# Attention and gated feed-forward on one core: x quarters on VectorE, sums tied to TensorE's order, and attention shifted between two phases

## The chip, the cores and the metric

The kernel runs on one core of one Trainium2 chip. The metric is device time in microseconds (us) of one execution. A core has TensorE (matrix products), VectorE, ScalarE and GpSimd, and SyncE, whose queue (SP) issues the transfers. Each engine executes its own instructions in the order in which they stand in the program; an instruction that has to wait holds back everything behind it on that engine. In the rows PE is TensorE, PEld its weight loads, DVE VectorE, ACT ScalarE, POOL GpSimd; SPq, PEq and so on are the queues that issue.

## The reference

```python
# attention over 8 batches, 8 heads, 576 positions of 64; keys and values averaged by 8 positions
k_p = k.reshape(B, H, Sp, 8, D).mean(axis=3)          # Sp = 72
v_p = v.reshape(B, H, Sp, 8, D).mean(axis=3)
scores = np.matmul(q, k_p.transpose(0, 1, 3, 2)) / np.sqrt(D)
scores = scores - np.max(scores, axis=-1, keepdims=True)
attn = np.exp(scores)
attn = attn / (np.sum(attn, axis=-1, keepdims=True) + 1e-09)
x = np.matmul(attn, v_p).transpose(0, 2, 1, 3).reshape(B * S, H * D)   # 4608 x 512
# feed-forward
h = x @ w_in                                          # 512 x 2048
g = h * np.clip(h + 3.0, 0.0, 6.0) / 6.0
out = g @ w_out                                       # 2048 x 512
```

## The kernel before

**Precision.** TensorE works in the float32r type. A number is split in a high part (a copy that rounds) and a low part (the number less the high part), and a product is made as high by high, high by low and low by high: three products for one. So each operand costs ScalarE a copy (`hi`) and VectorE a subtraction (`lo`).

**Blocks.** The 4608 tokens are worked off in blocks of 512, 256 and then 384 (`BLOCKS`). Blocks 0 to 3 are plain: for each of 16 chunks f of the hidden width, `Step.h` multiplies x by w_in (line 806, product `psh`), `relu` (814), `gate` (818), `hi` (822) and `lo` (826) make the gated value, and `Step.out` multiplies it by w_out (836, `pso`). `run` goes through these steps of a block with a lag of 2 between h and out; `hooks` adds work behind certain steps.

**Super blocks.** Blocks 4 to 11 go in pairs, as four super blocks. Their product by w_in uses a Strassen-like scheme of seven products instead of eight. It needs seven operands made of quarters of x, x1 to x7 (`x_ops`: `mix` adds or subtracts quarters of 128x768 elements, line 961, on GpSimd; `split` makes high and low parts, lines 952 and 953), and seven sums of quarters of w_in (`sums_of`, lines 902 to 910), which are made once, in blocks 2 and 3, and stored to DRAM. `plain_of` stores the other parts of the weights there. A super block then has two phases. In the *products phase* 56 products groups of six (line 1032, `psx`) run over the list N1; `keep` (1012) copies a result, `plus` (1007) adds one, and `gate` (1001, 1002) makes g. In the *out phase* g is split (`split_g`, lines 1018 and 1019) and multiplied by w_out (1077), 16 chunks f for six tiles t of 128 tokens; at the end each tile goes from PSUM into an `o` tile (1083) and to DRAM (1084). `next_w` loads weights of the products phase from DRAM, three chunks ahead in four buffers (932); `next_w2` those of the out phase, also in four buffers (938). In the last five chunks f of an out phase (`TAIL`) the x operands of the next super block are made.

**Attention.** While block j is multiplied, the attention of later blocks is computed in small steps, which `Paced` puts between the products, some per slot: `scores` (product 436, maximum 440, exponential 444, reciprocal 460 and 461, division on GpSimd 472 and 478), `transposes` (542 to 565; `ahi`, `alo`, `arem` are the split results), and the products with the values (`av`, 612), whose result a ScalarE copy (614) puts into x. Beside them stand the loads of queries (217), keys (224) and values (252, 257), and the sums over eight positions of keys (`prep_k`, 238) and values (`prep_v`, 356), on VectorE. A super block has `att_steps(j + 2)` in its products phase and `att_steps(j + 3)` in its out phase.

**What sets the order.** The program is written in one order and then placed engine by engine by a scheduler with a model of time of its own, which may move an instruction ahead of others that wait. Two things bind it: the table `ORDER` up to step 3 of block 1, and `behind`, which says that one instruction stands after another, without a wait at run time. Before, `behind` is used outside of the table in one place, the stores of plain weights: each stands behind the last TensorE instruction that had been written when it was written.

**Buffers.** Tiles of keys, values and queries, value sums and the output tiles `o` share one ring of four (`ring`). The tile `wq` of the weight sums exists once.

Of the kernel before, what the change touches and what calls it, by code (L numbers as in the profile page):

```python
# [89 lines left out]
def attention_moe_kernel(  # L90
# [72 lines left out]

    def put_in_order():

        a, b = window
        last = {}

        def on(i, engine):
            return i.engine == engine and (i.opcode == "DMACopy") == (engine == mybir.EngineType.SP)  # L170

        for name, text in ORDER.items():
            engine = getattr(mybir.EngineType, name)
            mine = [i for i in traced[a:b] if on(i, engine)]
            numbers = []
            for part in text.split():
                x, _, y = part.partition("-")
                numbers += range(int(x), int(y or x) + 1)
            assert sorted(numbers) == list(range(len(mine)))
            for x, y in zip(numbers, numbers[1:]):  # L180
                behind(mine[y], mine[x].name)
            last[engine] = mine[numbers[-1]].name
        for i in traced[b:]:
            if i.engine in last and on(i, i.engine):
                behind(i, last[i.engine])
# [42 lines left out]
    def prep_k(b, p):  # L228
# [11 lines left out]
        )  # L240
        if i == two:
# [104 lines left out]
    def prep_v(b, p):  # L346
# [11 lines left out]
        )  # L358
        if p == NPAIR - 1:
# [536 lines left out]
    def sums_of(i, h):  # L896
# [4 lines left out]
        for r, w in enumerate(pair_of(i)):  # L901
            nc.vector.tensor_tensor(  # L902
                out=q[:, 2 * r : 2 * r + 2], in0=w[:, 0, :, half], in1=w[:, 1, :, half], op=ALU.add
            )
        for to, a, b, how in ((0, 0, 2, ALU.subtract), (2, 2, 3, ALU.add), (3, 3, 0, ALU.subtract), (1, 1, 3, ALU.subtract)):
            nc.vector.tensor_tensor(out=q[:, to], in0=q[:, a], in1=q[:, b], op=how)  # L906
# [5 lines left out]
    def store(to, src):  # L912

        last = next(i for i in reversed(traced) if i.engine == mybir.EngineType.PE)
        nc.sync.dma_start(to, src)
        behind(traced[-1], last.name)
# [18 lines left out]
    def next_w2(n):  # L935
        while (m := len(loaded2)) <= n + 3 and m < len(supers) * NF:
            loaded2[m] = late[1].tile([P, 2, DM], F32R, name="ws2", bufs=4)
            nc.sync.dma_start(loaded2[m].bitcast(F32), w2_dram[m % NF])
        return loaded2[n]
# [3 lines left out]
    def x_ops(j):  # L943
# [15 lines left out]
        def mix(to, p, q, how):  # L959
            def make():  # L960
                nc.gpsimd.tensor_tensor(out=to(), in0=p(), in1=q(), op=how)
# [26 lines left out]
    def super_block(n, j, first_att, second_att):  # L988
# [9 lines left out]
        def gate(src, i, k):  # L998

            r = late[1].tile([P, HALF], F32, name="r", bufs=NREL)  # L1000
# [21 lines left out]
        for m, (i, o) in enumerate(N1):  # L1022
# [6 lines left out]
            paced.slot()  # L1029
            for c in range(2):  # L1030
# [28 lines left out]
        for f in range(NF):  # L1059
# [3 lines left out]
            for t in range(NT2):  # L1063
# [16 lines left out]
                o = ring("o")[:, :DM]  # L1080
# [220 lines left out]
    for n, step in enumerate(make):  # L1301
        j, u = (2, 3 + 2 * n) if n < 7 else (3, n - 7)
        hooks[j].setdefault(u, []).append(step)
# [16 lines left out]
    for n, j in enumerate(supers):  # L1320
        last = n == len(supers) - 1
        super_block(n, j, [] if last else att_steps(j + 2), [] if last else att_steps(j + 3))
# [46 lines left out]
```

## Time and profile before

| | |
|---|---|
| median of 3 runs | 928.28 us (927.34 to 930.86) |
| profiled execution | 928.58 us, of it 926.8 us span |
| TensorE busy | 893.1 us, 96% of the span |
| VectorE, ScalarE, GpSimd busy | 577.5, 512.2, 113.0 us |
| mean granted TensorE clock | 0.992 |
| moved by DMA | 172.63 MB, 186 GB/s in the mean |

The profiled execution took 928.58 us as a run; its span goes from the first instruction to the last. A busy TensorE isn't TensorE at its peak: products are pipelined, so the rows show a single product of 384 columns as 341 ns, while twelve in a row take little more than six times as long. Plain blocks end at about 362 us of the span, the four super blocks at about 507, 650, 795 and 927 us.

### The profile page before, as it was taken

The numbers are of one execution on the slowest core, as the hardware profiler recorded it, in microseconds if no ns is written. First come the engines' busy times: TensorE is split into PE (matmuls) and PEld (weight loads), VectorE is DVE, ScalarE is ACT, GpSimd is POOL, SyncE is SP. The second block draws the span as 40 slices with busy tenths as digits, with TensorE's granted clock in tenths as the row PEclk, the third lists the DMA queues.
The fourth block names the chain that finished last, engine by engine and source line by source line (L and its number), as shares of the span: only waits on it lengthen the run. The fifth ranks groups of instructions, "written<-read, shape, count | busy, mean of one in ns | idle before, by whom it ended". The sixth has DMA issues, their size and how long they took to land.

```text
span 926.8 us, 14062 instructions
## 1 busy us (share of the span) xinstructions
PE 893.1 (96%) x4760; PEld 801.4 (86%) x4760; DVE 577.5 (62%) x1167; ACT 512.2 (55%) x1473; POOL 113.0 (12%) x184
## 2 busy tenths in 40 slices
PE   7999999999999979899999999999999999999998
PEld 7788888899799878898888899888989888999786
DVE  6999846686867785867435886426676436454321
ACT  5998665665556465666323867423666534344221
POOL 4100002111101231001002201003110103000000
PEclk9999999999999999999999999999999999999999
DMA  9960205166549554976435976534966433775332
GB/s 302 392 249 0 92 12 178 46 192 202 169 129 343 181 159 165 337 242 216 160 114 172 335 260 227 165 114 135 325 210 214 161 116 114 257 232 192 114 119 108
DMA packets 93527, 172.63 MB, mean 186 GB/s; under 512 B 12048, under 2 KB 50704, under 8 KB 93456
## 3 DMA queue, kind: packets, MB, share of 16 engines
q1 hardware_dynamic: 93312, 171.74, 55.8%
q8 instruction: 38, 0.62, 0.3%
q14 instruction: 33, 0.27, 0.1%
q10 hardware_dynamic: 144, 0.00, 0.0%
HBM read 139.20 MB, written 32.51 MB: 185 GB/s over the span
## 4 chain that ended last, share of the span: by engine, by line
PE 67%; DVE 13%; DMA 11%; ACT 4%; SPq 3%; issue 2%; DVEq 0%; POOL 0%; ACTq 0%
PE psx L1077 28%; PE psx L1032 20%; PE psh L806 7%; PE pso L836 7%; DMA ws<-wd 3%; DMA wd<-wq 3%; PE psa L612 3%; PE psa L436 2%; DVE vsum L356 2%; ACT e L444 2%; SPq L910 2%; DVE wq L906 1%; DVE wq L902 1%; DMA kst<-k_l 1%; DMA raw<-w_in_l 1%
## 5 line engine op out<-in xcount | busy, mean ns | idle before, releaser
L1032 PE MATMUL psx<-x,ws 128*128 128x384 f32 x1344 | 255.9, 341 | 9.9 <-DMA ws<-wd 6.0
L1032 PEld LDWEIGHTS psx<-x,ws 128*128 128x128 f32 x1344 | 234.0, 190 | 16.0 <-DVE g L1007 4.2
L1077 PE MATMUL psx<-ws,ghi 128*128 128x512 f32 (+1 forms) x800 | 236.7, 384 | 1.6 <-DVE g L1002 1.6
L1077 PEld LDWEIGHTS psx<-ws,ghi 128*128 128x128 f32 x800 | 146.3, 188 | 28.7 <-DVE g L1002 2.1
L806 PE MATMUL psh<-xhi,w 128*128 128x384 f32 (+2 forms) x520 | 148.4, 343 | 5.0 <-DVE g L818 5.0
L1077 PE MATMUL psx<-ws,glo 128*128 128x512 f32 (+1 forms) x400 | 147.7, 382 | 0.0
L836 PE MATMUL pso<-w,ghi 128*128 128x512 f32 x384 | 121.6, 403 | 0.0
L1019 DVE TENSOR_TENSOR glo<-g,ghi 128x768 fp32r<-128x768 f32 x64 | 66.0, 1037 | 88.1 <-ACT ghi L1018 81.2
L806 PEld LDWEIGHTS psh<-xhi,w 128*128 128x128 f32 x520 | 94.4, 190 | 12.7 <-DVE g L818 5.9
L1018 ACT CAST ghi<-g 128x768 fp32r<-128x768 f32 x64 | 52.9, 835 | 82.4 <-PE psx L1077 80.4
L444 ACT ACTIVATE e<-psa,mx 128x72 f32<-128x72 f32 x256 | 78.8, 326 | 21.9 <-DVE mx L440 19.6
L806 PE MATMUL psh<-xlo,w 128*128 128x384 f32 (+2 forms) x260 | 88.1, 339 | 0.1
L1077 PEld LDWEIGHTS psx<-ws,glo 128*128 128x128 f32 x400 | 74.9, 188 | 14.2
L1001 ACT ACTIVATE r<-g,small 128x384 f32<-128x384 f32 x96 | 56.2, 614 | 43.7 <-DVE g L1007 42.9
L472 POOL TENSOR_TENSOR a<-e,sm 128x256 f32<-128x256 f32 x60 | 40.0, 669 | 327.3 <-DVE sm L461 237.4
L836 PEld LDWEIGHTS pso<-w,ghi 128*128 128x128 f32 x384 | 69.1, 190 | 10.4
L836 PE MATMUL pso<-w,glo 128*128 128x512 f32 x192 | 73.7, 398 | 0.0
L1007 DVE TENSOR_TENSOR g<-psx,c 128x384 f32<-128x384 f32 x96 | 53.0, 554 | 30.5 <-PE psx L1032 27.3
L1012 ACT COPY c<-psx 128x384 f32<-128x384 f32 x96 | 43.4, 486 | 23.3 <-PE psx L1032 22.7
L1002 DVE SCALAR_TENSOR_TENSOR g<-r,g 128x384 f32<-128x384 f32 x96 | 52.0, 570 | 4.7 <-ACT r L1001 4.6
L444 ACT ACTIVATION_READ_ACCUMULATOR e<-psa,mx 128x1 f32 x256 | 54.1, 211 | 0.0
L806 PEld LDWEIGHTS psh<-xlo,w 128*128 128x128 f32 x260 | 49.4, 190 | 4.4 <-DVE xlo L591 0.4
(120 smaller groups left out, 1194.0 us busy)
## 6 DMA issues: line engine op xcount, KB each, us to landing
ws<-wd SPq DMA_DIRECT2D x112, 512.0 KB, 4.3
ws<-w2d SPq DMA_DIRECT2D x64, 512.0 KB, 3.3
out<-o SPq DMA_DIRECT2D x35, 256.0 KB, 3.1
raw<-w_in_l SPq DMA_DIRECT2D x16, 512.0 KB, 8.5
raw<-w_out_l SPq DMA_DIRECT2D x16, 512.0 KB, 9.4
wd<-wq SPq DMA_DIRECT2D x64, 128.0 KB, 2.0
w2d<-w SPq DMA_DIRECT2D x16, 512.0 KB, 4.3
kst<-k_l SPq DMA_DIRECT2D x28, 288.0 KB, 4.9
```

The source lines that it names most:

```text
L444: nc.scalar.activation(self.e[:, h], self.ps[:, h], AF.Exp, bias=self.mx[:, h : h + 1], accum_out=self.sm[:, h : h + 1])
L472: engine.tensor_tensor(out=self.a[:, : 4 * D].rearrange("p (h s) -> p h s", h=4), in0=e[:, :, :D], in1=sm[:, :, None].broadcast_to([P, 4, D]),
L806: nc.tensor.matmul(self.ps, l[f][:, c, :], r[:, c, :], start=c == 0 and i == 0, stop=c == NCC - 1 and i == 2)
L836: nc.tensor.matmul(pos, l, r, start=f == 0 and i == 0, stop=f == NF - 1 and i == 2)
L1001: nc.scalar.activation(r, src, AF.Relu, bias=half_low, scale=GSCALE / (6.0 * WSCALE))
L1002: nc.vector.scalar_tensor_tensor(out=g_of[i][:, k], in0=r, scalar=GSCALE, in1=src, op0=ALU.min, op1=ALU.mult)
L1007: nc.vector.tensor_tensor(out=g_of[i][:, k], in0=ps, in1=kept, op=ALU.add)
L1012: nc.scalar.copy(c, ps)
L1018: nc.scalar.copy(hi, g)
L1019: nc.vector.tensor_tensor(out=lo, in0=g, in1=hi.bitcast(F32), op=ALU.subtract)
L1032: nc.tensor.matmul(ps, w[:, l, c * P : (c + 1) * P], t[:, r, c], start=o in (1, 2, 5) and c == 0 and k == 0, stop=c == 1 and k == 2, skip_ ...
L1077: nc.tensor.matmul(pos, l, w[:, r, cols], start=f == 0 and k == 0, stop=end and k == 2)
```

## The change

It has six parts.

1. `after_products` puts the instruction just written behind the last TensorE instruction written before it. It is called after each sum of keys (`prep_k`) and values (`prep_v`), after the first two adds of each sum of weights (`sums_of`), after the stores (as before) and after the loads of `next_w2`. It acts from step 3 of block 1 on.
2. The sums of weights are hooked to every second step of blocks 2 and 3, eight in each. Before, seven stood at steps 3, 5, ... 15 of block 2 and nine at steps 0 to 8 of block 3.
3. The quarters of x are mixed by VectorE instead of GpSimd.
4. The first loads of w_out for the first super block are written into its products phase, ahead of the first product of pair 6.
5. The outputs of a super block use buffers of `ghi2`, `glo2` and `r` (the last made wider for it), not the ring.
6. The attention steps of both blocks are joined, and the first 36% stand in the products phase, 64% in the out phase.

```diff
+    def after_products():
+        if len(window) == 2:
+            behind(traced[-1], next(i for i in reversed(traced) if i.engine == mybir.EngineType.PE).name)
...
@@ prep_k, prep_v: behind the tensor_reduce; sums_of: behind the tensor_tensor of line 902
+        after_products()
...
     def store(to, src):
-        last = next(i for i in reversed(traced) if i.engine == mybir.EngineType.PE)
         nc.sync.dma_start(to, src)
-        behind(traced[-1], last.name)
+        after_products()
...
             nc.sync.dma_start(loaded2[m].bitcast(F32), w2_dram[m % NF])
+            after_products()
...
-                nc.gpsimd.tensor_tensor(out=to(), in0=p(), in1=q(), op=how)
+                nc.vector.tensor_tensor(out=to(), in0=p(), in1=q(), op=how)
...
-            r = late[1].tile([P, HALF], F32, name="r", bufs=NREL)
+            r = late[1].tile([P, DM], F32, name="r", tag="ro", bufs=NREL)[:, :HALF]
...
             paced.slot()
+            if n == 0 and i == NPR - 2 and o == 1:
+                next_w2(0)
...
-                o = ring("o")[:, :DM]
+                tag, size = ("ro", DM) if t >= 4 else (("ghi2", "glo2")[t % 2], 2 * HALF)
+                o = late[1].tile([P, size], F32, name="o", tag=tag, bufs=3)[:, :DM]
...
-        j, u = (2, 3 + 2 * n) if n < 7 else (3, n - 7)
-        hooks[j].setdefault(u, []).append(step)
+        hooks[2 + n // NPR].setdefault(2 * (n % NPR), []).append(step)
...
-        super_block(n, j, [] if last else att_steps(j + 2), [] if last else att_steps(j + 3))
+        att = [] if last else att_steps(j + 2) + att_steps(j + 3)
+        cut = int(0.36 * len(att))
+        super_block(n, j, att[:cut], att[cut:])
```

What it does to the order shows at three places. The line numbers of the changed kernel are higher, by 7 to 10. VectorE at the change from block 1 to block 2, before: `vsum` are sums of values, `alo` low parts of transposed attention tiles.

```order
L826 TENSOR_TENSOR glo<-g,ghi 128x256
L356 TENSOR_REDUCE vsum<-vst 128x64 x3
L554 TENSOR_TENSOR alo<-psa,ahi 128x2x128
L818 SCALAR_TENSOR_TENSOR g<-g,psh 128x256
L554 TENSOR_TENSOR alo<-psa,ahi 128x2x128
L356 TENSOR_REDUCE vsum<-vst 128x64
```

The same place in the changed kernel (`mx` is the maximum of scores):

```order
L561 TENSOR_TENSOR alo<-psa,ahi 128x2x128 x2
L833 TENSOR_TENSOR glo<-g,ghi 128x256
L572 TENSOR_TENSOR arem<-psa,arem 32x128
L825 SCALAR_TENSOR_TENSOR g<-g,psh 128x256
L572 TENSOR_TENSOR arem<-psa,arem 32x128
L833 TENSOR_TENSOR glo<-g,ghi 128x256
L825 SCALAR_TENSOR_TENSOR g<-g,psh 128x256
L833 TENSOR_TENSOR glo<-g,ghi 128x256
L362 TENSOR_REDUCE vsum<-vst 128x64
L447 TENSOR_REDUCE mx<-psa 128x4 x2
```

Three sums of values in a row ahead of `alo` have become single ones behind it. SP at the start of the first super block, before: `ws<-w2d` are loads of w_out, `ws<-wd` of the products phase.

```order
L842 DMA out<-o 128x512
L252 DMA vst<-v_l 128x512
L842 DMA out<-o 128x512 x2
L252 DMA vst<-v_l 128x512
L938 DMA ws_4831<-w2d_120 128x1024
L938 DMA ws_4833<-w2d_121 128x1024
L252 DMA vst<-v_l 128x512
L932 DMA ws<-wd_96 128x1024
L938 DMA ws_4835<-w2d_122 128x1024
L938 DMA ws_4837<-w2d_123 128x1024
L932 DMA ws<-wd_97 128x1024
```

SP there in the changed kernel:

```order
L849 DMA out<-o 128x512 x3
L258 DMA vst<-v_l 128x512 x2
L944 DMA ws_4596<-w2d_120 128x1024
L938 DMA ws<-wd_96 128x1024
L258 DMA vst<-v_l 128x512
L938 DMA ws<-wd_97 128x1024
L944 DMA ws_4598<-w2d_121 128x1024
L938 DMA ws<-wd_98 128x1024
L944 DMA ws_4600<-w2d_122 128x1024
L944 DMA ws_4602<-w2d_123 128x1024
```

The four loads of w_out no longer stand together ahead of `wd_97`; one does. VectorE at the end of the third super block, before (`x_...` are the x operands, `o` the evictions at the end of the out phase, `g_8512` the first result of the next super block):

```order
L953 TENSOR_TENSOR x_8439<-x,x_8439 128x384 x2
L1019 TENSOR_TENSOR glo_8376<-g_7682,ghi_8375 128x768
L953 TENSOR_TENSOR x_8385<-mid,x_8385 128x384 x2
L953 TENSOR_TENSOR x_8396<-x,x_8396 128x384 x2
L1019 TENSOR_TENSOR glo_8412<-g_7779,ghi_8411 128x768
L953 TENSOR_TENSOR x_8417<-x,x_8417 128x384 x2
L953 TENSOR_TENSOR x_8428<-x,x_8428 128x384 x2
L1019 TENSOR_TENSOR glo_8451<-g_7779,ghi_8450 128x768
L1083 COPY o<-psx 128x512 x3
L1007 TENSOR_TENSOR g_8512<-psx,c 128x384
```

VectorE there in the changed kernel (L968 are the quarters of x):

```order
L561 TENSOR_TENSOR alo<-psa,ahi 128x2x128 x2
L572 TENSOR_TENSOR arem<-psa,arem 32x128 x2
L1093 COPY o<-psx 128x512 x3
L960 TENSOR_TENSOR x_8439<-x,x_8439 128x384
L968 TENSOR_TENSOR mid<-x 128x768
L960 TENSOR_TENSOR x_8439<-x,x_8439 128x384
L968 TENSOR_TENSOR x<-x 128x768
L1014 TENSOR_TENSOR g_8512<-psx,c 128x384
L960 TENSOR_TENSOR x_8385<-mid,x_8385 128x384 x2
L968 TENSOR_TENSOR x<-x,mid 128x768
L960 TENSOR_TENSOR x_8396<-x,x_8396 128x384 x2
```

The x operands have moved from ahead of the evictions to behind them, into the first products of the next super block.

More of the change, by code (lines that the diff above doesn't have):

```diff
@@ L912, in store @@
     def store(to, src):
-        last = next(i for i in reversed(traced) if i.engine == mybir.EngineType.PE)
         nc.sync.dma_start(to, src)
-        behind(traced[-1], last.name)
+        after_products()
     def plain_of(i, n):
@@ L938, in next_w2 @@
             nc.sync.dma_start(loaded2[m].bitcast(F32), w2_dram[m % NF])
+            after_products()
         return loaded2[n]
```

## The prediction

> **What bounds the kernel now.** I read the page from its first part down. One row says that TensorE sets the pace, and the chain of waits says how far.
>
> ```profile
> span 926.8 us, 14062 instructions
> PE 893.1 (96%) x4760; PEld 801.4 (86%) x4760; DVE 577.5 (62%) x1167; ACT 512.2 (55%) x1473; POOL 113.0 (12%) x184
> PE 67%; DVE 13%; DMA 11%; ACT 4%; SPq 3%; issue 2%; DVEq 0%; POOL 0%; ACTq 0%
> ```
>
> TensorE is busy for 893.1 of 926.8 us. Only 67% of the chain that ended last is its own; the rest, 13% VectorE and 11% transfers before all else, are stretches in which TensorE stood behind somebody. A change that adds no product can gain only there. Two rows of the chain give TensorE's pace where nothing is in its way:
>
> ```profile
> 383.34 10.43 PE psx L1032 x60
> 452.12 23.15 PE psx L1077 x102
> ```
>
> A product over 384 columns takes 10.43/60 = 0.174 us, one over 512 columns 23.15/102 = 0.227 us. By the code a super block has 56 x 6 = 336 of the first and 16 x 6 x 3 = 288 of the second: 58.5 + 65.4 = 123.9 us without attention. The next view is the busy time of each engine by stage; columns are TensorE, its weight loads, VectorE, ScalarE, GpSimd, granted clock, DMA share, GB/s.
>
> ```profile
> 334.00:362.00 28.00, 26.86 (x134) 24.38 (x134) 16.91 (x48) 16.38 (x61) 4.00 (x8) 0.94 0.29 88
> 362.00:399.00 37.00, 32.93 (x182) 32.03 (x181) 29.93 (x58) 24.87 (x65) 2.40 (x7) 0.95 0.97 339
> 399.00:452.00 53.00, 51.29 (x288) 48.15 (x287) 34.37 (x80) 31.45 (x108) 6.82 (x14) 0.97 0.59 189
> 505.00:540.00 35.00, 33.59 (x196) 31.48 (x194) 27.75 (x59) 25.62 (x93) 6.24 (x12) 1.00 0.93 326
> 540.00:595.00 55.00, 53.97 (x304) 51.06 (x303) 37.23 (x88) 37.37 (x120) 7.20 (x15) 1.00 0.62 201
> 740.00:795.00 55.00, 55.00 (x254) 45.91 (x253) 25.73 (x35) 19.89 (x43) 10.40 (x7) 1.00 0.40 134
> 795.00:850.00 55.00, 54.26 (x315) 53.13 (x314) 27.16 (x50) 26.56 (x51) 0.00 (x0) 1.00 0.74 245
> ```
>
> An out phase (740 to 795) has no gap for TensorE, 55.00 of 55.00 us, with VectorE at 25.73 and ScalarE at 19.89. Gaps stand at the end of the blocks (334 to 362, 26.86 of 28), at the change to super blocks (362 to 399, 32.93 of 37, with the clock at 0.95 and the DMA share at 0.97), and in products phases (399 to 452 and 505 to 595); there VectorE has up to 27.75 of 35 us of work. The last super block (795 to 850), which has no attention, lacks 0.74 us.
>
> **The waits, one by one.** The timeline gives each wait of TensorE with what ended it (in brackets), and what VectorE or SP did then.
>
> ```profile
> 160.44 0.41 PE L542 MATMUL psa<-ident,a 128*128 128x128 f32 x2 [1.91 <-DVE alo L554]
> 157.03 2.94 DVE L356 TENSOR_REDUCE vsum<-vst 128x64 f32<-128x512 f32 x3
> 233.45 0.76 PE L436 MATMUL psa<-kbd,qt 128*128 128x144 f32 x4 [1.40 <-DVE alo L554]
> 231.28 1.04 DVE L356 TENSOR_REDUCE vsum<-vst 128x64 f32<-128x512 f32 x1 [1.17 <-DMA vst<-v_l]
> 674.42 4.46 PE L1032 MATMUL psx<-x,ws 128*128 128x384 f32 x24 [1.99 <-DVE g L1007]
> 671.53 1.05 DVE L356 TENSOR_REDUCE vsum<-vst 96x64 f32<-96x512 f32 x1 [1.66 <-DMA vst<-vr_l]
> ```
>
> In each pair TensorE waits for a result of VectorE (the low part of a transposed tile, or `plus` on line 1007) while VectorE is in, or waits for the load of, sums of values (line 356). These waits are 1.91, 1.40 and 1.99 us, 5.3 together.
>
> ```profile
> 325.45 0.45 PE L806 MATMUL psh<-xhi,w 128*128 128x384 f32 x1 [1.03 <-DVE g L818]
> 335.14 0.44 PE L806 MATMUL psh<-xhi,w 128*128 128x384 f32 x1 [3.78 <-DVE g L818]
> 335.00:340.00 5.00, 4.86 (x17) 4.63 (x18) 5.00 (x14) 3.21 (x13) 0.00 (x0) 0.66 0.26 86
> 310.91 0.76 DVE L902 TENSOR_TENSOR wq<-w 128x256 f32<-128x256 f32 x2 [1.42 <-DMA wd<-wq]
> 319.12 3.09 DVE L902 TENSOR_TENSOR wq<-w 128x256 f32<-128x256 f32 x2 [1.27 <-DMA wd<-wq]
> 330.17 2.38 DVE L902 TENSOR_TENSOR wq<-w 128x256 f32<-128x256 f32 x2
> 320.02 1.91 POOL L961 TENSOR_TENSOR x<-x 128x768 f32<-128x768 f32 x1
> ```
>
> At the end of block 3 TensorE waits 1.03 and 3.78 us for a gate (line 818) that stands behind sums of weights (line 902) and x splits on VectorE, and then has 0.66 of its clock for 5 us, another 1.7: 6.5 us. The two adds of one sum of weights that took 0.76 us at 310 took 3.09 and 2.38 in the stretch of GpSimd's x quarters, after 1.27 us of waiting for the tile's last transfer.
>
> ```profile
> 373.09 3.88 PE L1032 MATMUL psx<-x,ws 128*128 128x384 f32 x12 [3.78 <-DMA ws<-wd]
> 365.53 1.18 SPq L938 DMA_DIRECT2D ws<-w2d  x2
> 366.81 0.68 SPq L932 DMA_DIRECT2D ws<-wd  x1
> 366.81 10.32 DMA ws<-wd
> 422.65 0.41 PE L542 MATMUL psa<-ident,a 128*128 128x128 f32 x2 [1.06 <-DVE alo L554]
> 423.75 3.53 PE L1032 MATMUL psx<-x,ws 128*128 128x384 f32 x12 [0.58 <-DMA ws<-wd]
> 509.46 0.69 DVE L1083 COPY o<-psx 128x512 f32<-128x512 f32 x1 [2.98 <-DMA out<-o]
> ```
>
> At 369 it waits 3.78 us for `ws`, then takes 3.88 for twelve products (2.09 at the pace, 0.17 for the last one's end): 5.4. At 422 it is 1.06 + 0.58 + 1.27 = 2.9. At 505 to 595 the stage rows lack 1.41 and 1.03, 2.4, with evictions waiting for an output's transfer at 509. The seven places sum to 22.5 us.
>
> **The change, part by part.** Sums are made against the profiled execution, 928.58 us (span 926.8 and 1.8 around it); the median of the runs is 928.28, so 0.3 lies between.
>
> *Sums of keys and values behind TensorE's last issued work.* Nothing is added: 28 and 36 instructions stand later in VectorE's queue, among gates instead of in threes ahead of them. What waits for them, the next batch's keys and values, has its use a phase later. I take the three waits as gone: -5.3. That is the one bound; the other is +5.3, if a sum made too late holds scores back as often as it now holds splits.
>
> *Sums of weights, every second step of blocks 2 and 3.* Before, nine of sixteen stood in block 3's first nine steps, one a step; a step there is 12 products of 0.174 and 9 of 0.227, 4.1 us. They have one tile, so each waits for the transfers of the one before (the 1.27 us above), and pushes the gates, splits and values behind it back by as much; what was late ran on until 334. At one in 8.2 us the wait has 4.1 us more to pass in. The same 16 sums are made, at no more work.
>
> *x quarters on VectorE.* Sixteen instructions over 128x768.
>
> ```profile
> L1019 DVE TENSOR_TENSOR glo<-g,ghi 128x768 fp32r<-128x768 f32 x64 | 66.0, 1037 | 88.1 <-ACT ghi L1018 81.2
> L961 POOL TENSOR_TENSOR x<-x 128x768 f32<-128x768 f32 x8 | 16.2, 2029 | 1.1 <-DVE x L953 0.6
> L953 DVE TENSOR_TENSOR x<-mid,x 128x384 fp32r<-128x384 f32 x8 | 13.6, 1727 | 0.3 <-ACT x L952 0.3
> 494.74 0.55 DVE L953 TENSOR_TENSOR x<-x,x 128x384 fp32r<-128x384 f32 x1
> ```
>
> VectorE's only instruction over 128x768, line 1019, takes 1.04 us, and I take that: 16.6 us in all, 4.2 in each of four places (GpSimd's 2.03 is the upper bound, 0.55 for half the width the lower). Against it, the eight splits that meet GpSimd take 1.73 us where an undisturbed one takes 0.55, so 9.4 us come back, and 4.0 on the two pairs of line 902 above. VectorE is idle for 29 of 55 us in the out phase, which hides what is left; at a super block's end that cover is missing (below). On GpSimd the divisions of attention move up past the quarters, at no cost. With both parts I take 5.5 of the 6.5 us at block 3 as gone; 0 and 6.5 are the bounds. [...]
>
> *The first super block's loads.* `next_w2(0)` is called within the products phase and its transfers follow it; in SP's order one load of w2, not two and later four, stands ahead of the first two `ws`.
>
> ```profile
> ws<-wd SPq DMA_DIRECT2D x112, 512.0 KB, 4.3
> out<-o SPq DMA_DIRECT2D x35, 256.0 KB, 3.1
> vst<-v_l SPq DMA_DIRECT2D x24, 256.0 KB, 4.6
> ```
>
> w2 loads have the size of `ws`. Ahead of and with the second `ws` there were 3 out, 3 vst, 4 w2, 2 ws, 4.7 MB; now 3 out, 3 vst, 1 w2, 2 ws, 3.1 MB (at the later ends the six outputs follow each other, where a w2 load that waits for its buffer stood between the fourth and the fifth). At that stage's 339 GB/s the 1.6 MB are 4.7 us. The other three w2 stand between the next `ws`, so I take 3.0 of 5.4 us (bounds 0 and 5.4).
>
> *36% of attention in the products phase, 64% in out.* It takes a third of the q, k and v loads and of the small work out of the products phase, whose weights alone need 512 KB in 12 x 0.174 = 2.09 us. The wait at 422 has a `ws` behind value loads: I take 2.0 of 2.9. In the out phase, with weights at 512 KB in 18 x 0.227 = 4.1 us and VectorE half idle, I cost the added steps at nothing; if that cover is gone, waits like the 1.4 us above come in.
>
> *The end of a super block.* With attention spread to the end, the last products with values stand right at the end of the third super block, and near that of the first; the x chain starts only behind them and is now VectorE's alone. In its order it is: middle 1.04, split 0.55, quarter 1.04, `plus` 0.55, two splits 1.10, quarter 1.04, split 0.55 = 5.9 us, against 4.2 us of products (four groups of six at 0.174) that don't need it, less ScalarE's copies in parallel: 1.7 and, for the next operand, about 2 more. I take 4.0 at the third end, 3.5 at the first, 0 at the second, where 60 products (13.6 us) follow the attention. The outputs no longer share a ring with loads, so the 2.4 us at 505 are replaced, not added to: +1.1 and +4.0. The bounds are 0 and the whole chain plus 2 more, 7.9 each. [...]
>
> Sum: -5.3 - 5.5 - 3.0 - 2.0 + 1.1 + 4.0 = -10.7 us, 928.6 - 10.7 = 917.9; I say 918.
>
> **Rivals.** (a) *More.* The ends hide as well (the next operands are ready because attention really finishes ahead of its place in the order): without +1.1 and +4.0, 928.6 - 15.8 = 912.8. For it speaks that out phases show no gap; against it, that the order itself puts the last products there. (b) *No change.* The waits for transfers and at block 3 stay (5.5, 3.0, 2.0), since a DMA share of 0.97 and the same bytes remain: 928.6 - 10.7 + 10.5 = 928.4. The share speaks for it; that the 10.32 us transfer stood behind four loads not needed yet speaks against. (c) *Slower.* At all three ends TensorE waits for the whole x chain: 7.9 and 1.7 for the clock as at 335, 9.6 each, 28.8 less the 2.4 at 505, against 15.8 gained: 928.6 + 10.6 = 939.2. It decides from (15.8 + 2.4 + 4.6)/3 = 7.6 us an end on; against it stands the second end's 13.6 us of cover.
>
> **How the numbers follow.** A measurement of this kernel tells about 0.5% (4.6 us) from no change. The forecast has 0.58, (a) 0.16, (b) 0.17, (c) 0.09. The forecast's own range is 911 to 924, from its halves of the bounds. Leaving out (c) and the outer part of (a) and (b) gives 909 to 927. Faster: 0.58 and 0.16, less 0.01 for its edge: 0.73; same 0.18; slower 0.09.
>
> **What would show it.** Right: no wait of TensorE behind sums of keys or values; L902 at 0.4 us each throughout and no split of 1.7; block 3 without a gap over 1 us; the second `ws` of the first super block landing in under 7 us; x quarters on VectorE near 1.04 us. At 1.7 us and more of wait for an x operand after the first and third out phases the end terms hold; at none, (a). Wrong: gaps in the out phases, splits of g late because of attention, or a wait over 6 us at an end.

## The result and the profile after

The changed kernel takes 915.97 us (median of 4 runs, 914.83 to 916.56) against 928.41 (927.34 to 930.86) for the kernel before in the same comparison: ratio 0.9861, 95% interval 0.9839 to 0.9883. The forecast was 918. The profiled execution took 916.45 us, 914.7 of it span. The page's first rows and the shares of the chain:

```profile
span 914.7 us, 14060 instructions
PE 889.2 (97%) x4760; PEld 797.4 (87%) x4760; DVE 569.7 (62%) x1183; ACT 515.6 (56%) x1473; POOL 82.9 (9%) x168
PE 86%; DVE 6%; DMA 4%; ACT 1%; SPq 1%; issue 1%; DVEq 0%; ACTq 0%
```

TensorE does the same 4760 products in 12.1 us less span, and its own share of the chain has gone from 67 to 86%. VectorE's share fell from 13 to 6%, that of transfers from 11 to 4%: the time came out of waits for both, and in part out of the clock (last section).

What is left shows in the timeline of TensorE (start, length, instructions, then in brackets the wait before them and what ended it):

```profile
332.69 0.44 PE L813 MATMUL psh<-xhi,w 128*128 128x384 f32 x1 [0.31 <-DVE g L825]
...
362.94 0.70 PE L1086 MATMUL psx<-ws,ghi 128*128 128x512 f32 x2 [1.41 <-DMA ws<-w2d]
364.81 3.88 PE L1041 MATMUL psx<-x,ws 128*128 128x384 f32 x12 [1.17 <-DMA ws<-wd]
...
507.19 3.40 PE L1041 MATMUL psx<-x,ws 128*128 128x384 f32 x18 [0.31 <-ACT c L1019]
...
784.70 1.51 PE L1041 MATMUL psx<-x,ws 128*128 128x384 f32 x7 [0.54 <-DVE g L1014]
786.97 1.32 PE L1041 MATMUL psx<-x,ws 128*128 128x384 f32 x6 [0.76 <-DVE x L960]
788.86 2.18 PE L1041 MATMUL psx<-x,ws 128*128 128x384 f32 x11 [0.57 <-ACT c L1019]
791.61 6.53 PE L1041 MATMUL psx<-x,ws 128*128 128x384 f32 x36 [0.57 <-ACT c L1019]
```

None of the three waits behind sums of values is there any more (160, 233 and 674 us before). Block 3 has 0.31 us where it had 1.03 and 3.78. The change to super blocks still has two waits and twelve products at 3.88 us. The first end of a super block has 0.31, the third has four waits, 2.44 us together.

For a full account I use a figure by stage: the length of a stage less what its products take at the prediction's paces (0.174 us for 384 columns, 0.227 for 512; for narrower ones 0.117 for 256, 0.094 for 192, 0.11 for 144 and 128, the spacing of undisturbed rows). A stage ends with the last eviction row of its block. What is left is TensorE time lost, an estimate good to about half a microsecond, from one profiled execution of each kernel; e1 to e12 are the experiments below. B1 to B3 are blocks 1 to 3, S1 to S4 the super blocks; the last column is when block 0 ended.

| kernel | median us | ratio to before, 95% | B1 | B2 | B3 | S1 | S2 | S3 | S4 | block 0 ends |
|---|---|---|---|---|---|---|---|---|---|---|
| before | 928.41 | | 5.0 | 4.6 | 8.0 | 11.2 | 5.0 | 5.0 | 4.1 | 142.3 |
| after | 915.97 | 0.984-0.988 | 0.7 | 4.5 | 2.5 | 9.0 | 2.5 | 3.2 | 6.1 | 144.6 |
| e1 sums of k, v free | 917.24 | 0.985-0.991 | 5.7 | 4.0 | 1.4 | 12.5 | 0.9 | 4.2 | 3.5 | 141.9 |
| e2 old hooks | 919.20 | 0.987-0.993 | 0.7 | 1.5 | 4.3 | 15.4 | 2.3 | 2.7 | 6.3 | 142.3 |
| e3 quarters on GpSimd | 926.46 | 0.996-1.000 | 0.7 | 6.3 | 4.9 | 4.7 | 7.1 | 3.1 | 11.3 | 143.3 |
| e4 attention in halves | 907.40 | 0.974-0.979 | 0.7 | 6.9 | 2.9 | 5.3 | 1.3 | 2.1 | 3.4 | 142.3 |
| e5 w_out loads anchored | 912.89 | 0.981-0.986 | 0.7 | 5.7 | 2.5 | 5.6 | 2.1 | 3.8 | 5.9 | 143.1 |
| e6 outputs in the ring | 917.20 | 0.986-0.990 | 0.7 | 6.4 | 2.7 | 6.8 | 4.1 | 4.0 | 7.1 | 142.7 |
| e7 before, quarters moved | 921.76 | 0.991-0.996 | 5.0 | 3.3 | 5.1 | 11.2 | 3.7 | 7.2 | 4.6 | 143.8 |
| e8 as e4, sums closer | 911.39 | 0.980-0.984 | 0.7 | 7.0 | 5.6 | 6.0 | 1.3 | 1.6 | 2.7 | 143.5 |
| e9 as e5, third in halves | 908.78 | 0.977-0.982 | 0.7 | 6.7 | 2.5 | 4.8 | 2.2 | 1.6 | 3.2 | 142.0 |
| e10 as e5, 43% | 908.53 | 0.977-0.981 | 0.7 | 7.0 | 2.5 | 4.6 | 2.3 | 1.5 | 3.1 | 141.6 |
| e11 as e5, 57% | 906.49 | 0.975-0.979 | 0.7 | 6.7 | 2.9 | 2.8 | 1.6 | 1.6 | 2.6 | 143.3 |
| e12 no early w_out loads | 915.43 | 0.983-0.989 | 0.7 | 5.4 | 2.8 | 11.4 | 1.7 | 2.4 | 7.3 | 142.8 |

From before to after the stages give -4.3, -0.1, -5.5, -2.2, -2.5, -1.8 and +2.0, together -14.4; block 0 ended 2.3 us later; -12.1 is the difference of the spans. Block 0, where the order is written out and the same in all of them, ends between 141.6 and 144.6 us: that much is chance from one execution to the next. (In the changed kernel's profile TensorE's granted clock was 0.51 from 13.5 to 17.0 us, 1.7 of its 2.3.) B2 varies between 4.5 and 7.0 among the eight kernels that differ only behind it (after, e4 to e6, e9 to e12), and it goes against block 0: the end of block 0 and the loss in B2 together come to 148.2 to 150.0 in all eight. What block 0 loses, B2 mostly gives back, so the two have to be read together.

### The profile page after: what moved, and what is told of

Its sections match the earlier page's. It is cut to its first block, busy times and chain, and to the rows that moved or that the text cites. A ratio compares the mean times of both kernels' runs of the same rounds, so it can differ in the third digit from the quotient of the medians.

```text
span 914.7 us, 14060 instructions
## 1 busy us (share of the span) xinstructions
PE 889.2 (97%) x4760; PEld 797.4 (87%) x4760; DVE 569.7 (62%) x1183; ACT 515.6 (56%) x1473; POOL 82.9 (9%) x168
## 4 chain that ended last, share of the span: by engine, by line
PE 86%; DVE 6%; DMA 4%; ACT 1%; SPq 1%; issue 1%; DVEq 0%; ACTq 0%
PE psx L1086 29%; PE psx L1041 24%; PE psh L813 12%; PE pso L843 12%; PE psa L619 3%; PE psa L443 3%; DMA ws<-wd 2%; PE psa L549 1%; DMA wd<-wq 1%; DMA stage<-v_l 1%; DVE x L960 1%; SPq L918 1%; PE psa L320 1%; DVE vsum L362 1%; DVE wq L916 0%
## 5 line engine op out<-in xcount | busy, mean ns | idle before, releaser
L1041 PE MATMUL psx<-x,ws 128*128 128x384 f32 x1344 | 249.4, 339 | 5.7 <-DMA ws<-wd 2.3
L1086 PE MATMUL psx<-ws,ghi 128*128 128x512 f32 (+1 forms) x800 | 239.2, 386 | 4.8 <-DVE g L1009 2.6
L813 PE MATMUL psh<-xhi,w 128*128 128x384 f32 (+2 forms) x520 | 146.1, 339 | 0.3 <-DVE g L825 0.3
L1026 DVE TENSOR_TENSOR glo<-g,ghi 128x768 fp32r<-128x768 f32 x64 | 61.5, 965 | 74.0 <-ACT ghi L1025 68.7
L1009 DVE SCALAR_TENSOR_TENSOR g<-r,psx 128x384 f32<-128x384 f32 x32 | 17.7, 553 | 62.7 <-ACT r L1008 62.5
```

The costliest lines, as they stand in the source:

```text
L813: nc.tensor.matmul(self.ps, l[f][:, c, :], r[:, c, :], start=c == 0 and i == 0, stop=c == NCC - 1 and i == 2)
L1009: nc.vector.scalar_tensor_tensor(out=g_of[i][:, k], in0=r, scalar=GSCALE, in1=src, op0=ALU.min, op1=ALU.mult)
L1026: nc.vector.tensor_tensor(out=lo, in0=g, in1=hi.bitcast(F32), op=ALU.subtract)
L1041: nc.tensor.matmul(ps, w[:, l, c * P : (c + 1) * P], t[:, r, c], start=o in (1, 2, 5) and c == 0 and k == 0, stop=c == 1 and k == 2, skip_ ...
L1086: nc.tensor.matmul(pos, l, w[:, r, cols], start=f == 0 and k == 0, stop=end and k == 2)
```

## The experiments

Line numbers of e1 and of e5 with those built on it are a few lower than in the changed kernel. A median within about 2.5 us of 915.97 can't be told from the changed kernel by time alone; there the rows decide.

**e1: sums of keys and values without their ordering.**

```diff
             out=ks[:, i], in_=kraw.pop((b, p)).rearrange("p (s o) -> p s o", o=POOL), axis=AX.X, op=ALU.add
         )
-        after_products()
@@ and the same call in prep_v
```

> The changed kernel without the ordering of the sums of keys and values (part 1 without prep_k and prep_v). Theory (these sums, placed in threes ahead of the low parts of attention tiles, held back TensorE): the three waits at 160, 233 and 674 come back with a row of line 356 ahead of them on VectorE, 5.3 us in all: about 921 us (919 to 923). Rival (the new attention split and the new places of the other sums had already moved the sums away from the tiles): no wait over 1 us behind them, 916 us.

Measured 917.24 us. The sums are back in threes, in front of what TensorE waits for. Rows of VectorE and TensorE at two places:

```profile
156.65 2.92 DVE L361 TENSOR_REDUCE vsum<-vst 128x64 f32<-128x512 f32 x3
160.04 0.41 PE L547 MATMUL psa<-ident,a 128*128 128x128 f32 x2 [1.95 <-DVE alo L559]
...
430.87 1.00 DVE L361 TENSOR_REDUCE vsum<-vst 128x64 f32<-128x512 f32 x1
432.39 0.73 PE L1084 MATMUL psx<-ws,ghi 128*128 128x512 f32 x2 [1.63 <-DVE g L1007]
```

B1 loses 5.0 us more, S1 3.5 and S3 1.0. Only the wait at 160 is back where the theory had it; at 233 there is none, and the loss in S1, around 432, is at a place that it did not name. The rival falls all the same, for it had no wait over 1 us behind these sums. The time is below the theory's 919 to 923, since the same edit let the scheduler place other work. By the order 72 products of w_out instead of none now stand behind the last product with values at the third end, and S4 loses 3.5 instead of 6.1; S2 loses 1.6 less and B3 1.1 less, for reasons that these rows don't show. The mechanism holds by its rows; an undo of one ordering isn't a measure of its worth, since the order around it changes too.

**e2: sums of weights at their old hooks.**

```diff
-        hooks[2 + n // NPR].setdefault(2 * (n % NPR), []).append(step)
+        j, u = (2, 3 + 2 * n) if n < 7 else (3, n - 7)
+        hooks[j].setdefault(u, []).append(step)
```

> The changed kernel with the sums of weights hooked as before (seven in block 2, nine at steps 0 to 8 of block 3), everything else changed. Theory (the end of block 3 was late because nine sums stood in a row, each waiting for the one weight tile): most of the 6.5 us at 325 to 340 come back, 4 to 6.5: 920 to 922 us. Rival (it was late because VectorE and GpSimd collided there; x quarters now on VectorE, so the old places do no harm): under 1.5 us, 916 to 917.5 us, and the two adds of one sum at 0.8 us throughout.

Measured 919.20: 3.2 us back, between the two. The place was not the one I named. Block 3 gets 1.8 us worse; the larger loss, 6.4, falls into S1, in part by the clock (0.51 from 358.0 to 365.0 and from 371.75 to 375.25). Rows of VectorE, ScalarE and TensorE:

```profile
356.34 0.76 DVE L909 TENSOR_TENSOR wq<-w 128x256 f32<-128x256 f32 x2 [2.04 <-DMA wd<-wq]
358.48 0.62 ACT L915 CAST wq<-wq 128x512 fp32r<-128x512 f32 x1 [4.50 <-DVE wq L914]
359.12 0.86 ACT L1019 COPY c<-psx 128x384 f32<-128x384 f32 x2
359.65 8.94 PE L1041 MATMUL psx<-x,ws 128*128 128x384 f32 x36 [5.69 <-ACT c L1019]
```

The last sum is still being made at 356 us, behind the end of block 3. ScalarE waits 4.50 us with its copy of `wq` (line 915), behind it stands the copy `c` of a result (1019), and TensorE waits 5.69 us for that copy. With one tile, two sums never start closer than 7.0 us to each other in any of these traces; nine of them hooked to nine steps of 4.1 us therefore run on far beyond their hooks.

**e3: x quarters on GpSimd again.**

```diff
-                nc.vector.tensor_tensor(out=to(), in0=p(), in1=q(), op=how)
+                nc.gpsimd.tensor_tensor(out=to(), in0=p(), in1=q(), op=how)
```

> The changed kernel with the x quarters on GpSimd again, everything else changed. Theory (two causes at block 3, each worth a part; at the other ends the quarters are a chain of 2.03 us each in place of 0.95): splits of x next to a quarter take 1.7 us again, 1 to 3 us come back at the end of block 3, and the third end waits 2 to 4 us more than the changed kernel's 2.4: 919 to 922 us. Rival 1 (the collision alone made block 3 late): all of 6.5 us there, 922 us and more. Rival 2 (the move bought nothing at block 3, and VectorE's own queue makes the wait at the third end): block 3 without a gap and the third end's 2.4 us gone, 913 to 914 us.

Measured 926.46: 10.5 us back, more than the theory gave. The first rival's "922 us and more" covers the time, but not by its reason, for block 3 takes only 2.4 of it. The groups of the changed kernel, then of e3 (busy time, mean ns of one):

```profile
L968 DVE TENSOR_TENSOR x<-x 128x768 f32<-128x768 f32 x8 | 7.6, 950 | 0.0
L960 DVE TENSOR_TENSOR x<-mid,x 128x384 fp32r<-128x384 f32 x8 | 4.2, 550 | 0.0
L909 DVE TENSOR_TENSOR wq<-w 128x256 f32<-128x256 f32 x32 | 12.9, 442 | 14.7 <-DMA wd<-wq 14.7
```

```profile
L968 POOL TENSOR_TENSOR x<-x 128x768 f32<-128x768 f32 x8 | 16.2, 2025 | 1.0 <-DVE x L960 0.6
L960 DVE TENSOR_TENSOR x<-mid,x 128x384 fp32r<-128x384 f32 x8 | 12.9, 1653 | 0.0
L909 DVE TENSOR_TENSOR wq<-w 128x256 f32<-128x256 f32 x32 | 16.0, 538 | 18.2 <-DMA wd<-wq 18.2
```

and TensorE's waits at the first and third end:

```profile
506.49 1.19 PE L1041 MATMUL psx<-x,ws 128*128 128x384 f32 x5 [2.20 <-DVE x L960]
793.91 4.95 PE L1041 MATMUL psx<-x,ws 128*128 128x384 f32 x17 [3.96 <-DVE x L960]
```

A quarter takes 2.03 us there for 0.95 on VectorE, and splits of `mid` beside it 1.65 for 0.55. VectorE's three groups that grew most (these by 8.7 us, the other splits by 5.2, line 909 by 3.1) sum to 17.0 us, about half of the 32.1 us of quarters on GpSimd beside them. With attention running to the end of the out phase the chain of quarters and splits is exposed, and made twice as slow it costs 4.6 us more in S2 and 5.2 in S4; B3 takes 2.4. The clock is part of these figures: it was 0.51 from 330.0 to 333.5, from 507.5 to 511.0 and from 790.75 to 797.75, and fell at none of these places in the changed kernel. Against them S1 loses 4.3 less: here the first load of w_out goes out at 364.09, behind four loads of the weights needed there. That is the matter of e4 and e5.

**e4: attention split as before.**

```diff
-        att = [] if last else att_steps(j + 2) + att_steps(j + 3)
-        cut = int(0.36 * len(att))
-        super_block(n, j, att[:cut], att[cut:])
+        super_block(n, j, [] if last else att_steps(j + 2), [] if last else att_steps(j + 3))
```

> The changed kernel with attention split as before: att_steps(j + 2) in the products phase, att_steps(j + 3) in the out phase. Theory (the split moved loads and VectorE work out of the products phases): the wait at 422 comes back with 2 to 3 us, those in the first 45 us of the second super block with 1 to 2.4, and the third end's 2.4 us go, since attention finishes earlier: net +1 to +3, 917 to 919 us. Rival (the split was worth nothing in itself: the wait at 422 went with the loads of w_out and the outputs off the ring): the third end's wait goes and nothing comes back, 913.5 us.

Measured 907.40, 8.6 us less than the changed kernel and outside both expectations: part 6, as it stands, costs. S4 gains 2.7 (no wait at the third end), S1 3.7. The second I had not foreseen. SP's rows for the first loads of w_out, of the changed kernel and of e4:

```profile
357.69 0.48 SPq L944 DMA_DIRECT2D ws<-w2d  x1
358.27 0.38 SPq L938 DMA_DIRECT2D ws<-wd  x1
359.65 0.75 SPq L944 DMA_DIRECT2D ws<-w2d  x1
361.12 1.57 SPq L944 DMA_DIRECT2D ws<-w2d  x2
```

```profile
397.47 0.42 SPq L944 DMA_DIRECT2D ws<-w2d  x1
```

In the changed kernel the four loads go out at 357.7 to 362.7 among the weights that are needed there; in e4 at 397 and behind. The call stands at the same place of the program. `after_products` puts the loads behind the last TensorE instruction written, and `paced.slot()` is called just ahead of it: with the 36% split that instruction is a transpose of an attention tile (`psa_4586<-ident_76,ar_4145`, line 551) which the scheduler had placed behind only 12 of the 336 products of this phase; with the old split it is a product with values, placed behind 246 of them.

**e5: the anchor mended.** The call goes behind the products of its group, so that the last instruction written is one of those.

```diff
-            if n == 0 and i == NPR - 2 and o == 1:
-                next_w2(0)
             for c in range(2):
...
+            if n == 0 and i == NPR - 2 and o == 1:
+                next_w2(0)
             if o in (1, 5, 6):
```

> The changed kernel with the early call of next_w2(0) moved behind the products of pair 6's first group, so that its loads stand behind a product of line 1041 and not behind whatever attention step was written last. Theory (in the changed kernel that step had itself been placed early, so the four loads of w_out share the change to super blocks with the weights that are needed there): the waits of 1.41 and 1.17 us at 363 to 365 shrink to one of 1.0 to 1.4, no twelve products at 3.9 us, 3 to 4 us less than the changed kernel: 912 to 913 us. Rival (the weights come late there because of outputs and value loads ahead of them on SP, whatever w_out does): 915.5 to 916.5 us.

Measured 912.89, as the theory said. TensorE at the same place, with no wait for `ws` and twelve products at the pace:

```profile
361.92 2.32 PE L1039 MATMUL psx<-x,ws 128*128 128x384 f32 x12 [0.65 <-DVE g L1014]
```

The stage loses 5.6 for 9.0. Half of that is the clock: it was 0.52 from 365.0 to 368.5 in the changed kernel and did not fall here. A later wait for `ws`, 1.38 us at 408, is new. The rival (outputs and value loads hold the weights up) falls: those transfers are there as before. The runs of the two kernels overlap by one of e5's (909.81 to 916.10, and 914.83 to 916.56), so the rows carry this more than the medians.

**e6: outputs in the ring again.**

```diff
-                tag, size = ("ro", DM) if t >= 4 else (("ghi2", "glo2")[t % 2], 2 * HALF)
-                o = late[1].tile([P, size], F32, name="o", tag=tag, bufs=3)[:, :DM]
+                o = ring("o")[:, :DM]
@@ and r as narrow as before
```

> The changed kernel with the outputs o back in the ring of four that keys, values and queries use (part 5 undone). Theory (the ring made outputs and loads wait for each other at 505 to 595): 2 to 2.4 us come back in the 90 us behind the end of the first super block, 918 to 918.5 us. Rival (with attention's loads at the new places the ring has room): no more than 0.5 us, 916 to 916.5 us.

Measured 917.20, between the two and not told from the changed kernel. Its rows have waits for weights that the changed kernel lacks, the first in S2, the second in S3:

```profile
509.91 1.30 PE L1041 MATMUL psx<-x,ws 128*128 128x384 f32 x6 [0.77 <-DMA ws<-wd]
653.28 3.40 PE L1041 MATMUL psx<-x,ws 128*128 128x384 f32 x18 [0.99 <-DMA ws<-wd]
```

S2 loses 1.6 us more, S3 0.8 and S4 1.0, S1 2.2 less; the clock did not fall there. The theory's effect shows in S2 at two thirds of its size; the median alone doesn't show it. That the ring itself holds these weights up is argued: four loads of keys stand among the outputs there (495 to 512 us), where the changed kernel has none, and a load of weights takes 5.7 us to land in the median for 3.4.

**e7: the kernel before with only the x quarters moved.**

```diff
-                nc.gpsimd.tensor_tensor(out=to(), in0=p(), in1=q(), op=how)
+                nc.vector.tensor_tensor(out=to(), in0=p(), in1=q(), op=how)
```

> The kernel before with only the x quarters on VectorE (part 3 alone). Theory (the move was worth 10.5 us with the new attention split because there the chain of x operands is exposed at two ends; with the old split that chain lies under other work, and only the end of block 3 gains): 2 to 4.5 us less than before, 924 to 926 us, TensorE's wait at 335 between 0 and 2 us. Rival 1 (the move is worth its 10 us anywhere): 918 us. Rival 2 (nine sums in a row alone make block 3 late): 927 to 928.5 us.

Measured 921.76, from 919.39 to 926.78 in eight runs: 6.5 us less, between the theory and the first rival. The profile is from the run at 926.78. B3 loses 2.9 us less, S2 1.3 less. Rows of TensorE:

```profile
332.16 0.45 PE L806 MATMUL psh<-xhi,w 128*128 128x384 f32 x1 [1.61 <-DVE g L818]
338.55 0.44 PE L806 MATMUL psh<-xhi,w 128*128 128x384 f32 x1 [0.90 <-DVE g L818]
370.17 6.00 PE L1032 MATMUL psx<-x,ws 128*128 128x384 f32 x18 [3.73 <-DVE vsum L356]
```

1.61 and 0.90 for 1.03 and 3.78 in block 3. The 3.73 us at 370 are the change to super blocks, as before. The row names a sum of values, but that one ended only 0.1 us behind the landing of the weights that the product also waits for. They are issued at 362.63, behind two loads of w_out, and take 7.4 us:

```profile
362.63 0.61 SPq L932 DMA_DIRECT2D ws<-wd  x1
```

This profile is the slowest of the eight runs; that the median gains more than it accounts for stays open.

**e8: e4 with the sums of weights closer together.**

```diff
-        hooks[2 + n // NPR].setdefault(2 * (n % NPR), []).append(step)
+        u = 15 * n // 8
+        hooks[2 + u // NF].setdefault(u % NF, []).append(step)
```

> The changed kernel with the old attention split, as in e4 (907.4 us), and the sixteen sums of weights hooked every 15/8 steps, so that the last one stands at step 12 of block 3 in place of 14. Theory (the stores of the last sum hold SP, behind them the outputs of block 3 and the first weights of the super block): the waits of 1.03 and 1.36 us at 355 and 363 shrink below 0.5 each, 905 to 906 us. Rival (SP waits there for the evictions of block 3 and not for the sums): 907 to 908 us, with the same two waits.

Measured 911.39, 4 us more than e4; both missed. The waits of 1.03 and 1.36 us at 355 and 363 went, as the theory had it. But B3 loses 5.6 for 2.9, by a gate behind a sum that waits for its tile, and by the clock, which was 0.51 from 337.0 to 340.5. Rows of VectorE and TensorE:

```profile
334.98 0.76 DVE L909 TENSOR_TENSOR wq<-w 128x256 f32<-128x256 f32 x2 [1.08 <-DMA wd<-wq]
336.77 0.44 PE L813 MATMUL psh<-xhi,w 128*128 128x384 f32 x1 [1.80 <-DVE g L825]
```

At a spacing of 7.7 us the sums come up against their single tile again. By this trace, in which no two sums start closer than 7.1 us, the 8.2 us of the change are close to the least that one tile allows.

**e9, e10, e11: how much attention stands in the products phase,** all with e5's anchor:

```diff
-        cut = int(0.36 * len(att))
+        cut = int((0.36 if n < 2 else 0.5) * len(att))    # e9
+        cut = int(0.43 * len(att))                        # e10
+        cut = int(0.57 * len(att))                        # e11
```

> e5 (anchor of the w_out loads mended, 912.9 us) with the attention before the third super block split in halves again, 36% kept for the first two. By the order 81 products of the out phase then stand behind the last one with values at the third end (18.4 us at 0.227), 14 in e5 (3.2 us). Theory (the chain of x operands is exposed at an end when fewer products than it lasts, some 9 us or 40 products, stand behind the last one with values): the 2.4 us of waits at the third end go and nothing else moves, 909 to 910.5 us. Rival (the third end's waits are VectorE's evictions and x operands in one queue, wherever attention stands): 912.5 to 913.5 us.

> e5 with 43% of attention in the products phase in all super blocks. By the order 25, 60 and 63 products stand behind the last one with values at the three ends (9, 60 and 14 in e5). Theory: the third end's 2.4 us go, the rest stays: 909 to 910.5 us. Rival (what the halves gain is spread over the products and out phases in proportion to the share): halfway between e5 and e4, 910.5 us, with the third end's waits still over 1 us.

> e5 with 57% of attention in the products phase, more than the half of e4 (907.4 us). 105 products stand behind the last one with values at all three ends, so the ends have nothing left to gain. Theory (products phases have less room: weights alone need 512 KB in 2.09 us, and VectorE has most of its work there): waits of 1 to 3 us in all in the products phases, 908.5 to 911 us. Rival (the less attention in the out phase the better): 905 to 907 us.

Measured 908.78, 908.53 and 906.49. In e9 and e10 the third end's waits are gone: S4 loses 3.2 and 3.1 for 5.9, S3 ahead of it 1.6 and 1.5 for 3.8. The theory of the exposed chain holds, and e10's rival with waits left over falls. Both times are a little below the theory's, since S3's 2.2 were not in it; what S3 gains by is not shown. The 14 of the expectations is a miscount: those products stand ahead of the last two groups of values. In e5's trace the last product with w_out ends at 776.22 and the last with values starts at 777.27, so that none stands behind it. Busy time at the third end, of the changed kernel and of e9 (columns as before: TensorE, its weight loads, VectorE, ScalarE, GpSimd, clock, DMA share, GB/s):

```profile
785.00:795.00 10.00, 8.10 (x43) 7.13 (x42) 8.59 (x18) 6.26 (x13) 0.00 (x0) 1.00 0.45 158
```

```profile
785.00:795.00 10.00, 10.00 (x63) 10.00 (x62) 6.16 (x10) 5.71 (x11) 0.00 (x0) 1.00 0.63 202
```

8.10 of 10 us busy with 43 products there, 10.00 with 63 here. In e11 the rival won: with 57% of attention in the products phases the only wait over 0.44 us in them is one of 1.07 at the end of block 3, which e4 has too (another of 0.77 stands ahead of the first product of an out phase, at 573.83), and S1 has the least loss of all (2.8). It is the best version found, 906.49 us, ratio 0.977, 95% interval 0.975 to 0.979; from e4 (907.40) it can't be told.

**e12: no early loads of w_out.** The ordering in `next_w2` stays.

```diff
-            if n == 0 and i == NPR - 2 and o == 1:
-                next_w2(0)
```

> The changed kernel without the early call of next_w2(0) (part 4 undone, its ordering behind products kept). By the order the first four loads of w_out then stand behind all but one of the weights of the first products phase. Theory (the loads leave the change to super blocks, as in e5, but now come late for the first out phase): 3 to 4 us gained at 363 to 365 and a wait of 1 to 3 us for w_out at about 440 us, 913.5 to 916 us. Rival (they still land in time, the early call is worth nothing): 912 to 913.3 us.

Measured 915.43, within the theory's range and 2.5 us above e5. The wait that it expected came, on SP and TensorE:

```profile
416.20 2.62 SPq L944 DMA_DIRECT2D ws<-w2d  x4
422.36 1.22 PE L1084 MATMUL psx<-ws,ghi 128*128 128x512 f32 x2 [1.33 <-DMA ws<-w2d]
```

1.33 us for the first load of w_out, and the clock was 0.50 from 423 to 428 behind it. So by these rows the early call has a use once its loads stand where it was written. Its size is not settled: the runs here reach from 910.09 to 918.14, those of e5 from 909.81 to 916.10, and the profile is of the slowest one.

## Why the total was right, and which of its steps were not

The forecast was -10.7 us and 918; -12.4 was measured. The total was right in part by luck: of six terms three held in their mechanism and three did not, and the errors cancelled. The range of 911 to 924 does not come out of the bounds given: half of the way to each, all taken one way, reaches from about 912 to 933.

- *Sums of keys and values* (-5.3): the three waits went, and e1 shows the mechanism, but the places were mis-sized. B1 gives 4.3 for 1.9: behind the wait at 160 the clock was 0.51 from 161.75 to 165.25, which the term left out (last section). S3 gives 1.8 for 2.0. B2 and block 0, read together, lose 2.2 more where 1.4 was to be gained. In all that is 3.9 for 5.3. A fourth place of the same kind, which I had put to another cause, stands in S1 (below).
- *Block 3* (-5.5): B3 gives 5.5. Both causes count, as said: the old hooks alone bring 1.8 back there, the quarters on GpSimd 2.4. What I had not seen is that late sums do their largest damage behind the block's end (e2).
- *x quarters*: 0.95 us, not 1.04, and the eight splits went from 1.73 to 0.55 as said. The 1.04 held collisions with GpSimd: before, three of the 64 instructions on line 1019 (at 490.81, 633.62 and 775.44) take 2.60 us for a median of 0.96, and each starts 0.3 us behind the start of a quarter there; in e7, where only the quarters have left GpSimd, the same line takes 961 ns in the mean. "L902 at 0.4 us each throughout" holds but for one pair of 1.25 us at 283.7 and a single one of 0.62 at 189.5.
- *First super block's loads* (-3.0): failed. "Its transfers follow it" is the step: I read the place of the call in the code and one load of w_out for two in SP's order, and took the other three as out of the way. They weren't, and I left out TensorE's order, which has a product with w_out at 363 that waits for the first of them. The two waits and the slow twelve products cost 1.41 + 1.17 + 1.62 = 4.2 us for 5.4, a gain of 1.2 and not 3.0; e5 shows what the place could give beyond that, 3.4 in S1.
- *36% and 64%* (-2.0): failed. The wait at 422 is gone, but not for this reason: e11, with 57%, has none there either. I put it to loads and a fuller VectorE and left out what VectorE did ahead of that `alo`. It is the kernel before once more:

```profile
421.15 1.03 DVE L356 TENSOR_REDUCE vsum<-vst 128x64 f32<-128x512 f32 x1 [2.75 <-DMA vst<-v_l]
422.09 0.41 DVE L554 TENSOR_TENSOR alo<-psa,ahi 128x256 fp32r<-128x256 f32 x1
```

  The low part stands behind a sum of values that waits 2.75 us for its load, the pattern of the other three; in e1 sums come back into that stage, and with them 3.5 us. As a whole the split costs 6.4 us (e5 against e11).
- *First end* (+3.5 against the 2.4 there before): failed, S2 gained 2.5. In the changed kernel the quarter `mid` starts at 495.27, two microseconds ahead of the end of the out phase, not behind it, and the next attention's scores stand among the first products. Only 0.31 us of the chain shows. Ten products with w_out stand behind the last one with values here; how much they covered and how much the scores did, no run separates:

```profile
495.27 0.96 DVE L968 TENSOR_TENSOR mid<-x 128x768 f32<-128x768 f32 x1 [0.47 <-ACT x L621]
498.59 0.65 PE L443 MATMUL psa<-kbd,qt 128*128 128x144 f32 x4
```

- *Third end* (+4.0): the mechanism held, the size was off: 2.44 us of waits, 2.0 by the stage. `mid` came at 781.89, behind the last product with values, which here stands behind all products with w_out (they end at 779.62), and the last super block has no attention to lie over it. The clock did not fall there (1.00 from 785 to 795).

```profile
780.68 0.34 PE L619 MATMUL psa<-arem,vrem 96*128 96x384 f32 x1
781.89 0.95 DVE L968 TENSOR_TENSOR mid<-x 128x768 f32<-128x768 f32 x1
```

Term by term, measured less forecast: +1.4 for the sums (with block 0), 0 for block 3, +2.8 for S1 (loads and split), -3.6 for the first end and -2.0 for the third: -1.4 on -10.7 gives the span's -12.1. Rival (a) had the first end right, rival (b) the transition; (c) needed 7.6 us at each end, and the largest was 2.4.

## What to carry to other kernels

An ordering "behind the last instruction written" is only as late as that instruction is placed: anchor it to work that stands where the call is written (worth 3.1 us here by the medians), and look in the order of the engine that waits, not only in that of the queue that loads. Before work is shifted out of one phase into the next, count what is left behind the last instruction of it that others need: with none the waits came to 2.4 us, with 63 there were none, and with ten, and other work among the next products, 0.3 us. Sums that share one buffer had a shortest spacing (7.0 us here), and hooks near it or below (7.7 us in e8, 4.1 in e2) only moved the damage to a later place.

## What the runs showed of the chip

TensorE's granted clock fell to about half (0.51) at some waits and stayed up at others that look the same. The wait at 160 was 1.91 us in the kernel before and 1.95 in e1, and in the 4.5 us up to 161.5 TensorE was busy for 2.59 and 2.55 us. Busy time and clock right behind it, of the kernel before and of e1:

```profile
161.50:165.50 4.00, 4.00 (x16) 3.20 (x15) 3.80 (x8) 2.20 (x6) 0.00 (x0) 0.57 0.55 150
```

```profile
161.50:165.50 4.00, 2.68 (x14) 1.76 (x12) 3.87 (x10) 2.47 (x7) 0.00 (x0) 1.00 0.44 130
```

The same at the change to super blocks, two stretches of the changed kernel and the second of them of e6, whose loads there are the same:

```profile
360.00:365.00 5.00, 2.43 (x12) 1.73 (x11) 3.51 (x7) 2.47 (x4) 0.00 (x0) 1.00 0.96 327
365.00:370.00 5.00, 5.00 (x21) 4.95 (x21) 0.00 (x0) 0.96 (x2) 0.00 (x0) 0.66 1.03 419
```

```profile
365.00:370.00 5.00, 5.00 (x30) 4.87 (x29) 0.94 (x3) 1.90 (x4) 0.00 (x0) 1.00 1.03 420
```

Behind the wait at 160 the clock was 0.57 in the mean in the one kernel and 1.00 in the other (where a second wait, 1.20 us at 164.59, makes up for it). At the change, TensorE was idle for 2.57 of 5 us in the changed kernel (waits of 1.41 and 1.17) and had 0.66 of its clock in the next 5; in e6, with waits of 1.05 and 1.14, it had 1.00. Elsewhere one wait of 2.30 us (e3, at 330) and one of 1.80 (e8, at 337) came with a fall, one of 2.33 (e9, at 363) did not, and the four waits of 0.54 to 0.76 us at the third end, 2.44 in 8 us, cost no clock.

In these traces a fall lasted 3.5 us at 0.51, in some places 7.0, which is about 1.7 us of TensorE's work for each 3.5. The profile of the kernel before has four (from 161.75, 335.75, 373.25 and 424.5), that of the changed kernel two (from 13.5 and 365.0), so by this estimate some 3.4 of the 12.1 us between the spans are clock.

Behind the wait of 3.73 us in e7 the clock was 0.50 from 370 to 375. But falls came at waits of 1.8 to 2.3 us as well (1.80 in e8, 1.91 in the kernel before, 2.30 in e3), and the pairs above show that neither the length of a wait nor the sum of several tells beforehand. What does tell, these runs leave open.
